# Two-bank PSUM tiles, 64-key post-mix matmuls and new planned durations in a talking-heads attention and MoE kernel

## The chip, the cores and the metric

The kernel runs on one core of a Trainium2 chip. The metric is the device time of one execution in microseconds (us); times before are the median of three runs, beside one profiled execution.

## The reference

All arrays are float32. Attention has batch 4, 12 heads, 448 positions, 64 features a head; the two feed-forward layers see 4 x 448 = 1792 tokens of 768 features, with hidden sizes 2048 and 1024.

```python
scores = scale * q @ k.T                                   # per batch and head
scores = einsum('bhij,hg->bgij', scores, w_pre)            # mixed across the 12 heads
attn = exp(scores - max(scores)); attn /= sum(attn) + 1e-9
attn = einsum('bhij,hg->bgij', attn, w_post)               # mixed across the heads again
x = (attn @ v) as [1792, 768]
h = x @ w_in;  x = elu(h) @ w_out                          # first layer, 768 -> 2048 -> 768
h = x @ w_in2; s = h * softmax(h); s = (s - mean) / sqrt(var + 1e-6) * g_ln
out = s @ w_out2                                           # second layer, 768 -> 1024 -> 768
```

## The kernel before

**Attention.** The 448 query rows of each batch are cut into chunks of 4 to 12 groups of 10 rows, 17 chunks in all (`CH`). For a chunk, a *score pair* (`add_score`, L428 to L461) computes the scores of two heads: four 64 x 64-tiled matmuls (L443) into two PSUM banks, one bank a head. Each bank is copied to SBUF by ScalarE or VectorE (L449, tile `sev`), and DMAs (*moves*, L454) bring the rows of all heads together into tile `sp`, so that the heads lie on partitions. A *unit* is two groups; there are 90. For each unit `pre` (L503 to L508) mixes the heads by matmuls into two banks (`pm`, for r = 0 and 1, five query rows each), `top` takes the maximum of each bank (L513, VectorE), `expo` the exponentials with their sums (L518, ScalarE), `guard`, `inv` and `weigh` (L522 to L531) put 1/sum into the post-mix weights `wr`. `post` (L532 to L542) mixes the heads again and transposes: for each of eight blocks of 56 keys (`JC`; the matmul covers 64, so that neighbours overlap by 8), each r and each of the unit's two groups there is one matmul with 64 keys as stationary columns. Its two output banks `po` hold four column blocks q with two partition halves x (block 2q + x). `take` copies them to `at` (L549). When all units of a chunk are done, `AV` multiplies with V: two halves of six heads (L590), 24 matmuls each, into one bank of the `sc` ring; each half is copied (L597) and stored to DRAM (L602, `xs`).

**PSUM.** The eight banks are three rings: `ps_sc` with three banks (score pairs and AV halves), `ps_po` with two, `ps_pm` with three. In chunks 0 and 1 score pairs also borrow `po` and `pm`.

**Order of work.** Attention's instructions are put in order by a list scheduler when the kernel is built (`schedule`, L296 to L352). Each `op` has a rank (a due time), what it depends on, the ring buffers it takes or uses, and a planned duration per engine that may run it. The scheduler takes the engine that can start earliest and on it the ready op of lowest rank; where two engines may do a copy, the one that would be done first, with `DA` added for VectorE against ScalarE. `tail` is the planned delay until another engine sees a result, `bufs` the size of each ring. Ranks come from a plan made of `PRE`, `POST`, `AV`, `SC` and `HID` (L361 to L393). Each engine and each DMA queue then works through its list in order.

**The first feed-forward layer** runs after it: for each of 8 feature groups `fg` and 4 token blocks `tb`, `hid` (two tiles of 18 matmuls, L256), `elu`, and `outp` of the block before (six tiles of 6 matmuls, L743), whose results VectorE adds up (L759). The two first hidden tiles (fg 0, tb 0) are scheduled by the planner as soon as their inputs are there. Hidden tiles take a bank of `ps_sc`, two of each eight one of `ps_h`. The weights of the second layer are decoded meanwhile (`decode`, L154 to L204: load, clamp L170, words, split, store to DRAM scratch `w2s`). These pieces wait in two lists, `urgent` and `later`; `tick` keeps up to three in progress, takes new ones from `urgent` first, and puts some of their steps between the matmul groups. All weights are decoded by the end of tb 2 of the last feature group (`drain(True)`, L788). **The second layer** loads the decoded weights with `w2_load` (L239 to L243): eleven of the 28 pieces in the last feature group, put on `urgent` at L786 behind tb 0, the others before the layer starts.

Of the kernel before, what the change touches and what calls it, by code (L numbers as in the profile page):

```python
# [26 lines left out]
WMAX = 120  # L27
JC = 56
# [10 lines left out]
XB = 2  # L39
# [13 lines left out]
DA = .4  # L53
T0 = 14
# [4 lines left out]
SB = 8  # L59
# [5 lines left out]
def kernel(ctx: ExitStack, tc: tile.TileContext, qa, kt, vt, wpre, wpost,  # L65
# [217 lines left out]
    tail = {"pe": .2, "act": .15, "dve": .15, "pool": .1, "sp": 2.0, "host": 0.0}  # L283
    bufs = {"sc": 3, "pm": 3, "po": 2, "sev": SB, "e": EB, "wr": WB, "st": 4, "kst": 2, "q": 4,
# [76 lines left out]
    PRE, POST, AV, SC, HID = .78, .96, 2.65, .78, 3.64  # L361
# [35 lines left out]
    k_op, q_op, av_op, sc_ev = {}, {}, {}, {}  # L397
# [30 lines left out]
    def add_score(c, h):  # L428
# [3 lines left out]
        ring = ("sc", "po", "pm")[h // 2 % 3] if c == 0 else ("sc", "po")[h // 2 % 2] if c == 1 else "sc"  # L432
        scb, svb = [Buf(ring) for _ in range(2)], [Buf("sev") for _ in range(2)]
# [3 lines left out]
        def mm(e):  # L437
            T[key] = [pools["ps_" + ring].tile([128, 512], F32, tag=ring, name="sc") for _ in range(2)]
            q, k = q_t[c, h // 6], kt_t[b, h]
            for x in range(2):  # L440
                for i in range(2):
                    sl = slice(64 * i, 64 * i + 64)
                    nc.tensor.matmul(T[key][i][64 * x:64 * x + 64, :S], q[sl, h % 6 // 2, 64 * x:64 * x + 64], k[sl, :],  # L443
                                     start=True, stop=True)

        def evac(e, i):
            t = T["sv", c, h + i] = (k0.tile([128, S], F32, name=f"s0_{h + i}") if c == 0 else
                                     sev_p.tile([128, S], F32, tag="sev", name="sev"))
            copier(e)(t, T[key][i][:, :S])  # L449
# [521 lines left out]
```

## Time and profile before

| what | value |
|---|---|
| median of three runs (lowest, highest) | 1116.82 us (1116.71, 1116.92) |
| the profiled execution, its own time | 1114.65 us |
| its span, first to last instruction | 1112.9 us |
| TensorE busy | 1071.1 us (96%) |
| VectorE, ScalarE, GpSimd busy | 724.0, 502.8, 238.3 us |
| mean granted TensorE clock | 0.986 |

A busy TensorE can still wait inside a group of matmuls, since matmuls overlap and their ends are modelled; so shares of busy time say less than the distance between the starts of groups. PE is TensorE's matmuls, PEld its weight loads, DVE VectorE, ACT ScalarE, POOL GpSimd, SP SyncE (its queue issues most DMAs); L with a number is a line of the kernel.

### The profile page before, as it was taken

The page shows a single profiled execution, that of the slowest core. Times are in us where ns is not written, and L with a number is a line of the kernel's source. Part 1 is how long each engine was busy: PE and PEld are TensorE (multiplying, and loading weights), DVE is VectorE, ACT ScalarE, POOL GpSimd, SP SyncE. Part 2 cuts the span into 40 slices and gives each one's busy share as a digit, 9 for nine tenths or more (in the row PEclk, how much of TensorE's full clock was granted, in tenths as well). Part 3 has the DMA queues.
Part 4 walks back from the last instruction along what each step waited for, and adds up shares of the span by engine and source line. Part 5 has one row for each costly group of instructions (what it writes and reads, how often), then busy time and mean ns, then how long its engine had stood idle before and what let it go on. Part 6 is the DMA issues. An engine that isn't in the chain of part 4 may idle for free.

```text
span 1112.9 us, 29821 instructions
## 1 busy us (share of the span) xinstructions
PE 1071.1 (96%) x12520; PEld 906.6 (81%) x12520; DVE 724.0 (65%) x1394; ACT 502.8 (45%) x1066; POOL 238.3 (21%) x251
## 2 busy tenths in 40 slices
PE   7899999999999899999999999999969999999998
PEld 2576667667776798998989999999969899898988
DVE  5586786677687457688878887878744553443532
ACT  3575677577675365333333434333321343333422
POOL 3210010011012325343344434333412000000000
PEclk8999999999999999999999999999999999999999
DMA  6775775775755432415234242424160600000001
GB/s 198 198 218 174 205 238 170 208 223 167 243 163 163 130 107 94 151 58 170 95 121 140 95 138 76 151 77 151 58 250 16 244 30 15 29 15 29 22 22 43
DMA packets 80232, 141.76 MB, mean 127 GB/s; under 512 B 21019, under 2 KB 59780, under 8 KB 80098
## 3 DMA queue, kind: packets, MB, share of 16 engines
q1 hardware_dynamic: 78275, 136.48, 38.5%
q0 software_dynamic: 896, 1.90, 0.7%
q8 instruction: 98, 1.61, 0.6%
q10 hardware_dynamic: 927, 1.48, 0.4%
q14 instruction: 36, 0.29, 0.1%
HBM read 75.96 MB, written 25.17 MB: 91 GB/s over the span
## 4 chain that ended last, share of the span: by engine, by line
PE 76%; DVE 10%; DMA 7%; issue 3%; ACT 3%; POOL 1%; SPq 0%; DVEq 0%; POOLq 0%; ACTq 0%
PE h L256 14%; PE o L743 14%; PE o L886 11%; PE h L839 11%; PE po L541 7%; PE sc L443 6%; PE pm L508 6%; PE av L590 6%; DMA sp<-sev 3%; DMA ws<-in_wo_dram 2%; DVE x L759 2%; DVE wy L184 1%; DMA ws<-in_wi_dram 1%; DVE wq L180 1%; PE tr L870 1%
## 5 line engine op out<-in xcount | busy, mean ns | idle before, releaser
L513 DVE TENSOR_REDUCE st<-pm 128x1 f32<-128x448 f32 x180 | 107.2, 617 | 72.5 <-PE pm L508 71.1
L743 PE MATMUL o<-gh,woh 128*128 128x448 f32 x384 | 142.2, 370 | 12.1 <-DVE x L759 10.2
L541 PEld LDWEIGHTS po<-wr,e 60*64 60x64 f32 x5760 | 115.2, 136 | 40.6 <-issue 26.6
L518 ACT ACTIVATE e<-pm,st 128x448 f32<-128x448 f32 x180 | 113.5, 634 | 65.2 <-DVE st L513 47.7
L743 PE MATMUL o<-gh,wol 128*128 128x448 f32 x384 | 140.7, 367 | 0.0
L743 PE MATMUL o<-glo,woh 128*128 128x448 f32 x384 | 140.7, 366 | 0.0
L269 POOL TENSOR_TENSOR glo<-g,gh 128x448 fp32r<-128x448 f32 x64 | 83.0, 1297 | 233.8 <-issue 125.1
L443 PE MATMUL sc<-kt,q 64*64 64x448 f32 x816 | 120.6, 564 | 4.6 <-DMA kt<-in_kt_dram 4.3
L541 PE MATMUL po<-wr,e 60*64 60x60 f32 x5760 | 118.9, 221 | 5.8 <-ACT at L549 2.6
L886 PE MATMUL o<-w,lh 128*128 128x384 f32 x448 | 120.3, 340 | 0.0
L508 PE MATMUL pm<-sp,wpre_t 64*64 64x448 f32 x720 | 107.9, 574 | 9.2 <-DMA sp<-sev 5.5
L839 PE MATMUL h<-w,x2h 128*128 128x512 f32 x336 | 107.7, 395 | 0.0
L759 DVE TENSOR_TENSOR x<-x,o 128x448 f32<-128x448 f32 x168 | 101.3, 611 | 8.7 <-PE o L743 8.7
L256 PE MATMUL h<-xh,wih 128*128 128x448 f32 x288 | 106.2, 369 | 0.0
L256 PE MATMUL h<-xl,wih 128*128 128x448 f32 x288 | 105.6, 367 | 0.0
L256 PE MATMUL h<-xh,wil 128*128 128x448 f32 x288 | 105.4, 366 | 0.0
L264 ACT ACTIVATE t<-t 128x448 f32<-128x448 f32 x64 | 37.0, 578 | 134.4 <-DVE t L263 134.4
L529 POOL TENSOR_TENSOR wr<-wpost_t,st 128x120 f32<-128x120 f32 x88 | 35.1, 399 | 288.7 <-DVE st L525 224.8
L590 PEld LDWEIGHTS av<-at,v 128*64 128x64 f32 x1632 | 76.2, 138 | 18.2 <-issue 6.6
L743 PEld LDWEIGHTS o<-gh,woh 128*128 128x128 f32 x384 | 72.6, 189 | 21.4 <-DVE x L759 13.1
L590 PE MATMUL av<-at,v 128*64 128x120 f32 (+5 forms) x1632 | 83.4, 259 | 6.4 <-ACT sev L449 3.3
L549 DVE COPY at<-po 128x480 f32<-128x480 f32 (+1 forms) x119 | 74.6, 649 | 14.9 <-PE po L541 14.1
(98 smaller groups left out, 1949.1 us busy)
## 6 DMA issues: line engine op xcount, KB each, us to landing
sp<-sev SPq DMA_DIRECT2D x94, 210.0 KB
ws<-in_wi_dram SPq DMA_DIRECT2D x33, 512.0 KB
ws<-in_wo_dram SPq DMA_DIRECT2D x21, 512.0 KB
q<-in_qa_dram SPq DMA_DIRECT2D x34, 192.0 KB
v<-in_vt_dram SPq DMA_DIRECT2D x24, 256.0 KB
w2s<-ws SPq DMA_DIRECT2D x12, 512.0 KB
ws<-in_wo_dram SPq DMA_DIRECT2D x16, 384.0 KB
w2s<-ws SPq DMA_DIRECT2D x16, 384.0 KB
```

Source lines behind the costliest of these rows:

```text
L256: nc.tensor.matmul(ps[:, :S], a[:, kc * FG + ft * 128:kc * FG + (ft + 1) * 128], x[:, kc, :], start=kc == 0 and n == 0, stop=kc == ECH - 1 ...
L269: nc.gpsimd.tensor_tensor(glo, g, f(gh), ALU.subtract)
L443: nc.tensor.matmul(T[key][i][64 * x:64 * x + 64, :S], q[sl, h % 6 // 2, 64 * x:64 * x + 64], k[sl, :], start=True, stop=True)
L508: nc.tensor.matmul(ps_t[u][r][64 * s:64 * s + 64, :S], wpre_t[p, :], sp_t[c][p, g, :], start=True, stop=True)
L513: nc.vector.tensor_reduce(out=st_t[u][:P, r:r + 1], in_=ps_t[u][r][:P, :S], op=ALU.max, axis=AX.X, negate=True)
L518: nc.scalar.activation(out=t[:P], in_=ps_t[u][r][:P, :S], func=AF.Exp, bias=st[:P, r:r + 1], scale=1.0, accum_out=st[:P, 2 + r:3 + r])
L541: nc.tensor.matmul(out[:, :, 5 * r:5 * r + 5], e_t[u, r][sl, j:j + 64], wr_t[u][sl, r].rearrange("p (g a) -> p g a", a=5), start=True, sto ...
L590: nc.tensor.matmul(ps[64 * k:64 * k + 64, i, :], v_t[CH[c][0]][:, 6 * n + 2 * i + k, q, :], at_t[c][:, q, 6 * n + 2 * i + k, :w], start=q ...
L743: nc.tensor.matmul(ps[:, :S], a[:, ft * DM + e * 128:ft * DM + (e + 1) * 128], x, start=n == 0, stop=n == 5)
L759: nc.vector.tensor_tensor(x1[tb][:, e, :], x1[tb][:, e, :], ps[:, :S], ALU.add)
L839: nc.tensor.matmul(ps[:, hf * 512:hf * 512 + 512], a[:, k, :], w, start=n == 0, stop=n == 3 * ECH - 1)
L886: nc.tensor.matmul(ps[:, :384], a[:, k, :], w, start=n == 0, stop=n == 3 * FC - 1)
```

## The change

- `post` works on seven blocks of 64 keys in place of eight overlapping ones: blocks 0 to 5 lie in column blocks q = 0 to 2 as before; block 6 is computed for r = 0 in partition half 0 and for r = 1 in half 1 of q = 3. The other places of q = 3 are zero from two memsets at the start, and V's last block holds the same keys in both halves. `po` is two fixed tiles instead of a ring.
- A score pair is one tile of two banks, and the ring `sc` holds one such tile. From chunk 1 on the pair is emptied by one copy into one `sev` tile for two heads (four of these instead of eight of one head). Chunk 0 uses the rings `sc`, `pm`, `pm` and copies head by head; chunk 1 uses `sc` alone.
- `pm` holds two tiles of two banks; one maximum instruction covers both.
- Both AV halves of a chunk go to one `sc` tile, with one copy and one store (`XB` from 2 to 1 buffer of double size).
- The first two hidden tiles take one `pm` tile and wait for the last `pre`; all others use a ring `ps_h` of four banks.
- Planned durations, `tail`, `DA`, the rings' sizes and V's first due times are new. Moves of chunks 0 and 1 may go to SP's or ScalarE's queue, those of chunk 2 to SP's or GpSimd's (before: chunk 0 SP or GpSimd, chunk 1 all three, chunk 2 SP or GpSimd).
- The eleven early `w2_load` go to the end of `later` instead of `urgent`.

```diff
-JC = 56
...
-XB = 2
+XB = 1
...
-DA = .4
+DA = 0
...
-SB = 8
+SB = 4
...
-    ps_sc = pool("ps_sc", 3, space=PSUM)
-    ps_po = pool("ps_po", 2, space=PSUM)
-    ps_pm = pool("ps_pm", 3, space=PSUM)
+    ps_sc = pool("ps_sc", 1, space=PSUM)
+    ps_po = pool("ps_po", 1, space=PSUM)
+    po_p = [ps_po.tile([128, 512], F32, name=f"po{i}") for i in range(2)]
+    ps_pm = pool("ps_pm", 2, space=PSUM)
...
-            ring, p = ("sc", ps_sc) if (tb, ft) not in ((1, 1), (3, 1)) else ("h", ps_h)
-            h_t[fg, tb, ft] = p.tile([128, 512], F32, tag=ring, name="h")
+            if (fg, tb) != (0, 0):
+                h_t[fg, tb, ft] = ps_h.tile([128, 512], F32, tag="h", name="h")
+            elif ft == 0:
+                t = ps_pm.tile([128, 2, 512], F32, tag="pm", name="h")
+                h_t[0, 0, 0], h_t[0, 0, 1] = t[:, 0], t[:, 1]
         ps = h_t[fg, tb, ft]
...
-    tail = {"pe": .2, "act": .15, "dve": .15, "pool": .1, "sp": 2.0, "host": 0.0}
-    bufs = {"sc": 3, "pm": 3, "po": 2, "sev": SB, "e": EB, "wr": WB, "st": 4, "kst": 2, "q": 4,
+    tail = {"pe": .3, "act": .2, "dve": .17, "pool": .1, "sp": 2.0, "host": 0.0}
+    bufs = {"sc": 1, "pm": 2, "po": 2, "sev": SB, "e": EB, "wr": WB, "st": 4, "kst": 2, "q": 4,
...
-    PRE, POST, AV, SC, HID = .78, .96, 2.65, .78, 3.64
+    PRE, POST, AV, SC, HID = .76, .83, 2.6, .76, 3.64
...
-        ring = ("sc", "po", "pm")[h // 2 % 3] if c == 0 else ("sc", "po")[h // 2 % 2] if c == 1 else "sc"
-        scb, svb = [Buf(ring) for _ in range(2)], [Buf("sev") for _ in range(2)]
+        ring = ("sc", "pm", "pm")[h // 2 % 3] if c == 0 else "sc"
+        scb, svb = Buf(ring), Buf("sev")
...
-            T[key] = [pools["ps_" + ring].tile([128, 512], F32, tag=ring, name="sc") for _ in range(2)]
+            T[key] = pools["ps_" + ring].tile([128, 2, 512], F32, tag=ring, name="sc")
...
+            t = T["sv", c, h + i] = k0.tile([128, S], F32, name=f"s0_{h + i}")
+            copier(e)(t, T[key][:, i, :S])
...
+        def evac(e):
+            t = sev_p.tile([128, 2, S], F32, tag="sev", name="sev")
+            T["sv", c, h], T["sv", c, h + 1] = t[:, 0], t[:, 1]
+            copier(e)(t, T[key][:, :, :S])
...
+                o2 = op(r + .9 + .1 * i, lambda e, i=i: evac0(e, i), [o1], [], [scb], act=.43, dve=.54)
...
+                o2 = op(r + .9, evac, [o1], sv, [scb], act=.8, dve=1.0)
...
-                sp_op.setdefault(c, []).append(op(r + 2 + .2 * i + .1 * n, lambda e, i=i, to=to: move(e, i, *to), [o2], [spb_[c]], sv, lag=3.5, sp=.78, **({"act": .78} if c == 1 else {}), **({"pool": 1.0} if c < 3 else {})))
+                sp_op.setdefault(c, []).append(op(r + 2 + .2 * i + .1 * n, lambda e, i=i, to=to: move(e, i, *to), [o2], [spb_[c]], sv if c else [], lag=3.5, sp=.78, **({"act": .78} if c < 2 else {"pool": 1.0} if c == 2 else {})))
...
+    for t in po_p:
+        nc.vector.memset(t, 0.0)
...
-        pmb, pob = [Buf("pm") for _ in range(2)], [Buf("po") for _ in range(2)]
+        pmb, pob = Buf("pm"), [Buf("po") for _ in range(2)]
...
-            ps_t[u] = [ps_pm.tile([128, 512], F32, tag="pm", name="pm") for _ in range(2)]
+            ps_t[u] = ps_pm.tile([128, 2, 512], F32, tag="pm", name="pm")
...
-        def top(e, r, u=u, P=P):
-            if r == 0:
-                st_t[u] = pools["st"].tile([128, 8], F32, tag="st", name="st")
-            nc.vector.tensor_reduce(out=st_t[u][:P, r:r + 1], in_=ps_t[u][r][:P, :S], op=ALU.max, axis=AX.X, negate=True)
+                    nc.tensor.matmul(ps_t[u][64 * s:64 * s + 64, r, :S], wpre_t[p, :], sp_t[c][p, g, :], start=True, stop=True)
+
+        def top(e, u=u, P=P):
+            st_t[u] = pools["st"].tile([128, 8], F32, tag="st", name="st")
+            nc.vector.tensor_reduce(out=st_t[u][:P, 0:2], in_=ps_t[u][:P, :, :S], op=ALU.max, axis=AX.X, negate=True)
...
-            ps = po_t[u] = [ps_po.tile([128, 512], F32, tag="po", name="po") for _ in range(ns)]
-            for q in range(4):
-                for r in range(2):
-                    for x in range(2):
-                        j = min((2 * q + x) * JC, S - 64)
-                        for s in range(ns):
-                            sl = slice(64 * s, 64 * s + 60)
-                            out = ps[s][64 * x:64 * x + 64, q * 120:q * 120 + 120].rearrange("p (g a) -> p g a", a=10)
-                            nc.tensor.matmul(out[:, :, 5 * r:5 * r + 5], e_t[u, r][sl, j:j + 64],
-                                             wr_t[u][sl, r].rearrange("p (g a) -> p g a", a=5), start=True, stop=True)
+
+
+            ps = po_t[u] = po_p
+            for todo in [[(r, 2 * q + x, q, x) for x in range(2)] for r in range(2) for q in range(3)] + [[(0, 6, 3, 0), (1, 6, 3, 1)]]:
+                for r, n, q, x in todo:
+                    for s in range(ns):
+                        sl = slice(64 * s, 64 * s + 60)
+                        out = ps[s][64 * x:64 * x + 64, q * 120:q * 120 + 120].rearrange("p (g a) -> p g a", a=10)
+                        nc.tensor.matmul(out[:, :, 5 * r:5 * r + 5], e_t[u, r][sl, 64 * n:64 * n + 64],
+                                         wr_t[u][sl, r].rearrange("p (g a) -> p g a", a=5), start=True, stop=True)
...
-        for r in range(2):
-            ot = op(r0 + .9 + .1 * r, lambda e, r=r, top=top: top(e, r), [o], [] if r else [sb], [pmb[r]] + ([sb] if r else []), dve=.62)
-            ex.append(op(r0 + 1.6 + .8 * r, lambda e, r=r, expo=expo: expo(e, r), [ot], [eb[r]], [pmb[r], sb], act=.84))
+        ot = op(r0 + .9, top, [o], [sb], [pmb], dve=1.0)
+        ex = [op(r0 + 1.6 + .8 * r, lambda e, r=r, expo=expo: expo(e, r), [ot], [eb[r]], [pmb, sb], act=.63) for r in range(2)]
+        o = op(r0 + 3.2, guard, ex, [], [sb], dve=.07)
+        o = op(r0 + 3.3, inv, [o], [], [sb], dve=.07)
+        ow = op(r0 + 3.4, weigh, [o, o_wpost], [wb], [sb], dve=.3, pool=.38)
...
-                                [pob[s]] + ([at_b[c]] if g else []), act=.58, dve=.64))
+                                [pob[s]] + ([at_b[c]] if g else []), act=.45, dve=.57))
...
-                ov.append(op(t_av[c, 0] - VD + 4 * i if b else T0 + 5 + 2 * i, lambda e, i=i, load=load: load(e, i), [o_begin], [] if i else [vb], [vb] if i else [], sp=.5, lag=4.0))
+                ov.append(op(t_av[c, 0] - VD + 4 * i if b else T0 + 8 + 2.5 * i, lambda e, i=i, load=load: load(e, i), [o_begin], [] if i else [vb], [vb] if i else [], sp=.5, lag=4.0))
+        xb, avb = Buf("x"), Buf("sc")
+
+        def mm(e, n, c=c, w=w):
+            if n == 0:
+                x_t[c] = ps_sc.tile([128, 2, 512], F32, tag="sc", name="av")
...
+        def take(e, c=c, w=w):
+            T["x", c] = pools["xt"].tile([128, 2, 3, WMAX], F32, tag="x", name="x")
+            copier(e)(T["x", c][:, :, :, :w], x_t[c][:, :, :3 * w].rearrange("p n (k w) -> p n k w", k=3))
...
-            o = op(r + AV + .2, take, [o], [xb], [avb], act=.45, dve=.5)
-            T["xs", c, n] = op(r + AV + 1, store, [o], [], [xb], sp=.5, more=.2)
+            o = op(t_av[c, n], lambda e, n=n, mm=mm: mm(e, n), at_ops[c] + ov + [o], [] if n else [avb], [vb, at_b[c]] + ([avb] if n else []), pe=AV * w / 120)
+        o = op(t_av[c, 1] + AV + .2, take, [o], [xb], [avb], act=.68, dve=.78)
+        T["xs", c, 0] = T["xs", c, 1] = op(t_av[c, 1] + AV + 1, store, [o], [], [xb], sp=.5, more=.2)
...
+    hb, o = Buf("pm"), None
     for ft in range(2):
-        o = None
         for p in range(3):
             o = op(t_hid + HD + ft * .01, lambda e, ft=ft, p=p: hid(0, 0, ft, range(2 * p, 2 * p + 2)),
-                   need + [o] + [sc_ev[lc, h] for h in range(NH)], pe=HID / 3)
+                   need + [o, pre_op[NU - 1]], [hb] if (ft, p) == (0, 0) else [], [hb], pe=HID / 3)
...
-    release("ps_pm", "ps_po")
+    release("ps_pm", "ps_po", "ps_sc")
...
-    ps_h = pool("ps_h", 1, space=PSUM)
+    ps_h = pool("ps_h", 4, space=PSUM)
...
-                    urgent.append([(0, lambda i=i: w2_load(i, p), 0)])
+                    later.append([(0, lambda i=i: w2_load(i, p), 0)])
...
-    vb = v.reshape(NB, NH, 4, 2, JC, D)
+    vb = v.reshape(NB, NH, 7, 64, D)
     for n in range(8):
-        o = 8 if n == 7 else 0
-        vt[:, n % 2, o:o + JC, :, n // 2] = vb[:, :, n // 2, n % 2].transpose(0, 2, 1, 3)
+        vt[:, n % 2, :, :, n // 2] = vb[:, :, min(n, 6)].transpose(0, 2, 1, 3)
```

## Rows read from the trace of the kernel before

**Rows 1.** Windows by stage: us, busy us and instructions of each engine, clock, DMA share, GB/s.
```profile
60.00:350.00 290.00, 282.00 (x7527) 205.47 (x7518) 211.93 (x535) 190.94 (x510) 30.92 (x78) 0.99 0.66 199
350.00:395.00 45.00, 39.73 (x683) 34.15 (x683) 25.41 (x42) 20.42 (x44) 15.72 (x12) 0.92 0.42 124
395.00:810.00 415.00, 411.64 (x2025) 378.83 (x2024) 326.24 (x534) 165.09 (x292) 165.09 (x124) 1.00 0.34 113
```

**Rows 2.** Chain that ended last, 232 to 256 us: start, us, what.
```profile
...
237.04 2.61 PE av L590 x48
239.65 0.91 PE pm L508 x8
240.56 0.93 PE po L541 x64
241.49 0.76 PE sc L443 x8
...
253.94 1.03 PE po L541 x63
```

**Rows 3.** Timeline of TensorE, 230 to 256 us; six score pairs, the first to the last.
```profile
241.31 0.94 PE L443 MATMUL sc<-kt,q 64*64 64x448 f32 x8
...
248.63 0.93 PE L443 MATMUL sc<-kt,q 64*64 64x448 f32 x7
...
250.00 1.23 PE L443 MATMUL sc<-kt,q 64*64 64x448 f32 x5
...
252.97 1.06 PE L443 MATMUL sc<-kt,q 64*64 64x448 f32 x8
...
254.90 1.35 PE L590 MATMUL av<-at,v 128*64 128x120 f32 x22
```

**Rows 4.** Groups by shape over the whole span: count, busy us, mean ns, idle before.
```profile
L541 PE MATMUL po<-wr,e 60*64 60x60 f32 x5760 | 118.9, 221 | 5.8 <-ACT at L549 2.6 <-issue 2.1 <-POOL wr L529 0.8
L518 ACT ACTIVATE e<-pm,st 128x448 f32<-128x448 f32 x180 | 113.5, 634 | 65.2 <-DVE st L513 47.7 <-DVE st L525 15.4 <-DVE st L522 1.9
L449 ACT COPY sev<-sc 128x448 f32<-128x448 f32 x129 | 65.3, 536 | 29.6 <-PE sc L443 11.3 <-DMA sp<-sev 8.9 <-DVE sev L449 2.4
L449 DVE COPY sev<-sc 128x448 f32<-128x448 f32 x63 | 38.7, 620 | 7.5 <-PE sc L443 5.2 <-ACT sev L449 1.1 <-ACT e L518 0.4
...
L848 DVE TENSOR_REDUCE s<-h 128x1 f32<-128x1024 f32 x14 | 17.1, 1224 | 77.4 <-PE h L839 77.4
L849 ACT ACTIVATE raw<-h,s 128x1024 f32<-128x1024 f32 x14 | 15.7, 1119 | 21.8 <-DVE s L848 21.6
```

**Rows 5.** Waits of TensorE's weight loads, 60 to 350 us: us, times, longest.
```profile
PEld sc L443 <- ACT sev L449: 6.5, 13, 1.1
```

**Rows 6.** Timeline of TensorE, 819 to 840 us, around its longest stop.
```profile
834.47 0.74 PE L743 MATMUL o<-gh,woh 128*128 128x448 f32 x1 [8.79 <-DVE x L759]
...
839.12 0.57 PE L256 MATMUL h<-xh,wih 128*128 128x448 f32 x1
```

**Rows 7.** Timeline of SP's queue, 780 to 840 us.
```profile
811.62 7.84 SPq L242 DMA_DIRECT2D w<-w2s  x11
820.42 0.33 SPq L161 DMA_DIRECT2D ws<-in_wo_dram  x1
```

**Rows 8.** Timeline of VectorE, 811 to 840 us.
```profile
830.32 0.36 DVE L170 TENSOR_SCALAR ws<-ws 128x384 f32<-128x384 f32 x1 [11.15 <-DMA ws<-in_wo_dram]
```

**Rows 9.** Timeline of all engines, 0 to 32 us.
```profile
1.93 4.54 DVE L470 MEMSET sp<- 128x5376 f32 x1 [1.93 <-issue]
4.27 14.02 PE L443 MATMUL sc<-kt,q 64*64 64x448 f32 x96 [4.27 <-DMA kt<-in_kt_dram]
```

**Rows 10.** Windows of undisturbed scores, and of the stop near 825 us.
```profile
300.00:340.00 40.00, 40.00 (x1134) 29.98 (x1132) 29.81 (x76) 26.99 (x72) 4.64 (x12) 1.00 0.57 174
820.00:830.00 10.00, 5.68 (x29) 4.92 (x27) 0.00 (x0) 0.00 (x0) 1.05 (x1) 0.97 1.01 405
830.00:840.00 10.00, 5.53 (x16) 4.94 (x17) 6.18 (x12) 2.72 (x5) 2.12 (x2) 0.52 0.12 47
```

More of the change, by code (lines that the diff above doesn't have):

```diff
@@ L442, in mm, with evac0 @@
                     sl = slice(64 * i, 64 * i + 64)
-                    nc.tensor.matmul(T[key][i][64 * x:64 * x + 64, :S], q[sl, h % 6 // 2, 64 * x:64 * x + 64], k[sl, :],
+                    nc.tensor.matmul(T[key][64 * x:64 * x + 64, i, :S], q[sl, h % 6 // 2, 64 * x:64 * x + 64], k[sl, :],
                                      start=True, stop=True)
[L446 to L449, printed above, removed]
+        def evac0(e, i):
+            t = T["sv", c, h + i] = k0.tile([128, S], F32, name=f"s0_{h + i}")
[4 more added lines that the diff above has]
+            copier(e)(t, T[key][:, :, :S])
         def move(e, i, p, r0, r1):
@@ L507, in pre @@
                     p = slice(64 * r, 64 * r + 64)
-                    nc.tensor.matmul(ps_t[u][r][64 * s:64 * s + 64, :S], wpre_t[p, :], sp_t[c][p, g, :], start=True, stop=True)
-        def top(e, r, u=u, P=P):
-            if r == 0:
-                st_t[u] = pools["st"].tile([128, 8], F32, tag="st", name="st")
-            nc.vector.tensor_reduce(out=st_t[u][:P, r:r + 1], in_=ps_t[u][r][:P, :S], op=ALU.max, axis=AX.X, negate=True)
+                    nc.tensor.matmul(ps_t[u][64 * s:64 * s + 64, r, :S], wpre_t[p, :], sp_t[c][p, g, :], start=True, stop=True)
+        def top(e, u=u, P=P):
+            st_t[u] = pools["st"].tile([128, 8], F32, tag="st", name="st")
+            nc.vector.tensor_reduce(out=st_t[u][:P, 0:2], in_=ps_t[u][:P, :, :S], op=ALU.max, axis=AX.X, negate=True)
         def expo(e, r, u=u, P=P):
@@ L517, in expo @@
             t = e_t[u, r] = pools["e"].tile([128, S], F32, tag="e", name="e")
-            nc.scalar.activation(out=t[:P], in_=ps_t[u][r][:P, :S], func=AF.Exp, bias=st[:P, r:r + 1], scale=1.0,
+            nc.scalar.activation(out=t[:P], in_=ps_t[u][:P, r, :S], func=AF.Exp, bias=st[:P, r:r + 1], scale=1.0,
                                  accum_out=st[:P, 2 + r:3 + r])
@@ L579 @@
             for i in range(6):
-                ov.append(op(t_av[c, 0] - VD + 4 * i if b else T0 + 5 + 2 * i, lambda e, i=i, load=load: load(e, i), [o_begin], [] if i else [vb], [vb] if i else [], sp=.5, lag=4.0))
-        for n in range(2):
-            r = t_av[c, n]
-            xb, avb = Buf("x"), Buf("sc")
-            def mm(e, c=c, n=n, w=w):
-                ps = x_t[c, n] = ps_sc.tile([128, 512], F32, tag="sc", name="av")[:, :3 * w].rearrange("p (k w) -> p k w", k=3)
-                for i in range(3):
-                    for q in range(4):
-                        for k in range(2):
-                            nc.tensor.matmul(ps[64 * k:64 * k + 64, i, :], v_t[CH[c][0]][:, 6 * n + 2 * i + k, q, :], at_t[c][:, q, 6 * n + 2 * i + k, :w],
-                                             start=q == 0, stop=q == 3)
-            o = op(r, mm, at_ops[c] + ov, [avb], [vb, at_b[c]], pe=AV * w / 120)
-            def take(e, c=c, n=n, w=w):
-                T["x", c, n] = pools["xt"].tile([128, 3, WMAX], F32, tag="x", name="x")
-                copier(e)(T["x", c, n][:, :, :w], x_t[c, n])
-            def store(e, c=c, n=n, w=w):
-                b, r, _ = CH[c]
-                dst = xs[b][n * 384:n * 384 + 384, r:r + w]
-                dma(dst.rearrange("(k p) w -> p k w", k=3), T["x", c, n][:, :, :w])
-            o = op(r + AV + .2, take, [o], [xb], [avb], act=.45, dve=.5)
-            T["xs", c, n] = op(r + AV + 1, store, [o], [], [xb], sp=.5, more=.2)
@@ new lines @@
+                ov.append(op(t_av[c, 0] - VD + 4 * i if b else T0 + 8 + 2.5 * i, lambda e, i=i, load=load: load(e, i), [o_begin], [] if i else [vb], [vb] if i else [], sp=.5, lag=4.0))
[3 more added lines that the diff above has]
+                x_t[c] = ps_sc.tile([128, 2, 512], F32, tag="sc", name="av")
+            for i in range(3):
+                for q in range(4):
+                    for k in range(2):
+                        h = 6 * n + 2 * i + k
+                        nc.tensor.matmul(x_t[c][64 * k:64 * k + 64, n, i * w:i * w + w], v_t[CH[c][0]][:, h, q, :], at_t[c][:, q, h, :w],
+                                         start=q == 0, stop=q == 3)
```

21 lines of the change are left out of this document (11 added, 10 removed).

## The prediction

> **What bounds the kernel now.** I read the table of windows first, since it splits the span by stage. From 60 to 350 us (attention) TensorE is busy 282 of 290 us, and from 395 to 810 us (the first feed-forward layer) 411.6 of 415; for long it stands idle only in 350 to 395 us, 5.3 us [rows 1], and once near 825 us, 8.8 us [rows 6]. In attention DMA has a share of 0.66, VectorE is busy 212 and ScalarE 191 of the 290 us, so none of these is full. A busy TensorE may still be one that is held up inside a group, so I read the chain of waits next: each group of matmuls starts where the one before it ended, av 2.61 us, pm 0.91, po 0.93, sc 0.76 [rows 2]. This stretch is bound by what TensorE has to issue, and a matmul taken away there is time gained, as long as no new wait appears. Third, the timeline of TensorE between two AV blocks shows how close the score pairs follow each other, because the change gives them one buffer in place of three banks. Last, I followed the idle time near 825 us from engine to engine.
>
> **Post-mix, 64 instead of 56 keys for each matmul.** The list of a unit goes from 4 x 2 x 2 x 2 = 32 matmuls to 7 x 2 x 2 = 28. The trace holds two instructions for each (5760 = 90 units x 64 [rows 4]), so 8 of 64 go. The chain takes 0.93 us for 64 [rows 2], 14.5 ns each; 8 x 14.5 ns x 90 units = 10.5 us. Bounds: 0 if the posts wait for weights or for a buffer whatever their number, and 11.8 us at the rate of the slower groups (1.03 us for 63 [rows 2], 16.3 ns x 8 x 90). I take 10.5: 0.93 is what a group takes that waits for nothing. AV still runs over four key blocks of 128 rows: its count does not change.
>
> **The score ring, three banks to one two-bank tile.** Before, a pair's two banks are emptied side by side, 0.536 us on ScalarE and 0.620 on VectorE [rows 4]. Afterwards one instruction empties 2 x 448 columns. The trace has none of this shape; its bounds are one 448-column copy and the 1024-column passes over a two-bank tile, 1.119 us on ScalarE and 1.224 on VectorE [rows 4]. Between these, VectorE needs 0.620 + 448 x (1.224 - 0.620)/576 = 1.09 us; ScalarE, with the slope of its own exps from 0.634 to 1.119, needs 0.536 + 448 x 0.842 ns = 0.91 us. The last matmul of a pair ends 0.94 us after the first one starts [rows 3]; with the copy that is 1.85 to 2.03 us, and with 0.2 us for the two handovers (my estimate, from the 0.15 us by which pm, right after an AV group, is longer in the chain than sc [rows 2]) a pair holds the only tile for 2.05 to 2.25 us. Six pairs start between 241.31 and 252.97 us [rows 3], 2.33 us apart in the mean: on average they fit. But the spacing is uneven: 248.63 and 250.00 are 1.37 apart, and the AV block follows the last pair by 1.93 us. Stretching two such spacings by 0.8 us and the last by 0.3 costs 1.9 us a chunk, 30 us over 16 chunks, if TensorE has nothing else to do in these gaps. The other end is 0: the planner orders by readiness, and each chunk has five or six pre and post groups of 0.8 us to put there. The row nearest to it is what TensorE's weight loads waited for score copies with three banks, 6.5 us in 13 waits [rows 5]. I take as much again, +6.5 us. Queued behind a waiting score matmul are the next pre and post, as TensorE takes its list in order; who waits for these are the VectorE maxima, and through them the copies, so a wait is handed on. For AV, both halves now share the score tile: it is held 5.2 us of matmuls and one copy of 720 columns, between 0.54 and 1.12 us by the same two rows, and the pre and post that follow an AV half (0.91 + 0.93 us) cover the copy. If that cover is gone it costs about 1 us a chunk, within the 30.
>
> A rule of the Trainium skill speaks against this part: "TensorEngine Tiling (Array Packing)", section "PSUM Bottleneck", says that packed matmuls leave the emptying of PSUM as the limit, and asks for both ScalarE and VectorE on it. The rows agree so far as one engine alone takes 0.91 us or more where two in parallel took 0.62. By the rule the sum would lie at the bad end, with 30 us in place of 6.5. [...]
>
> **Maxima, exps and copies.** One maximum over 896 columns (1.09 us by the slope above) replaces two of 448, at most 0.62 each if they cost what the VectorE copy of that shape does [rows 4]: 0.15 us less per unit at most, on an engine that is not full [rows 1]. I cost it at nothing; the first exp of a unit starts some 0.5 us later, and is hidden by the three units that pre runs ahead. The pm ring goes from three banks to two pairs, which removes the wait of a unit's second bank; nothing is counted for it.
>
> **W2 loads from the urgent list to the end of the later one.** Here TensorE stands from 825.7 to 834.47 us, 8.79 us, for an addition on VectorE [rows 6]. VectorE sat 11.15 us before a clamp at 830.32, waiting for a weight load; that load was issued at 820.42 on SP's queue, behind eleven W2 loads that took SP from 811.62 to 819.46 and fill the DMA engines (share 1.01 in 820 to 830 us) [rows 7, 8, 10]. Afterwards the last spill's load goes ahead of these eleven. Then TensorE restarts at the lower clock level: the 12 matmuls from 834.47 to 839.12 take 4.65 us [rows 6] where 12 at 0.203 (411.6 us for 2025 of them [rows 1]) take 2.44. Together 8.8 + 2.2 = 11.0 us. Bounds 0 (another late load takes the wait's place) and 11.0. I take 10. Late next are the W2 loads: eleven of 512 KB are 5.8 MB, 14 us at the 405 GB/s of that window [rows 10]. In the code they are wanted only after hid(7,3) and two more output groups, at the pace of rows 1 some 20 us after the stop's end, so they have cover; past that each costs its own 1.3 us.
>
> **Start and tail.** Two memsets of 128x512 by VectorE's 4.54 us for 128x5376 [rows 9] are 0.4 us each, in front of the first copies: +0.5 (0 to 1). Chunks 0 and 1 score twelve pairs in 14.0 us [rows 9] over all three rings; now chunk 1 has the one tile, 6 x 2.2 = 13.2 us by itself: +2 (0 to 4), since pre waits for the moves' DMA anyway. These 26 moves leave GpSimd's queue for SP and ScalarE, whose copies queue behind an issue (planned at 0.78 us): 0, give or take 3. At the tail the first hidden tiles use the pm ring and need the last pre; that stage's 5.3 us of idle [rows 1] can move by 3 either way. The first layer's four-bank h ring changes a stage where TensorE is 99% busy: 0. New planned durations shift every due time (0.02 + 0.13 us a unit, 0.02 a pair, 0.05 an AV half: about 17 us less in all); loads issue earlier, on an SP queue with room: 0, give or take 4.
>
> **Sum.** -10.5 + 6.5 - 10 + 0.5 + 2 = -11.5 us. The profiled execution took 1114.65 us (span 1112.9 and 1.75 around it), 2.2 below the median of 1116.82; the difference is taken off the median: 1105.
>
> **The rivals.**
> *The ring costs nothing.* The planner fills the gaps, and shorter copies take waits out of the chain. For it: mean spacing 2.33 against 2.25 needed. Both gains in full and start and tail even: 1116.8 - 10.5 - 11 = 1095. Chance 0.22.
> *The ring is the bound.* Place: the score stretch of each chunk; it decides from the point where pair plus copy exceeds the spacing that pre and post leave, about 2.3 us. A copy that queues 0.3 us behind an exp is enough. Full price 30: 1116.8 - 10.5 - 10 + 30 + 2.5 = 1129, the case reaching from 1118 up. Chance 0.15; the 1.37 us spacings speak for it, the mean against it.
> *The gains do not arrive.* Attention is held by the moves into sp instead (DMA share 0.66 [rows 1]), so fewer post matmuls only lengthen waits, or another late load takes the W2 wait's place: with one of the two gains lost and the ring's price, 1115, between 1111 and 1118. Chance 0.15.
> *The clock.* Waits of the ring could bring TensorE to its lower level. From 300 to 340 us, where score waits occur, the granted clock was 1.00; it was 0.52 after the 8.8 us stop [rows 10]. One fall per chunk at the 2.2 us of the W2 stop is 16 x 2.2 = 35 us, from 1105 to 1140. Chance 0.03. The Trainium skill, "TensorE: Matmul & The Clock Gate", section "A second HAM failure mode: psum-queue depth-cycling", says that cycling through PSUM banks can idle TensorE often enough for its clock to swing; this trace shows no such swing with sub-microsecond waits.
>
> **How the numbers follow.** The forecast of 1105 (its own range 1099 to 1111) has 0.45. A change under 0.2% (2.2 us) can't be told from none here. Faster, below 1114.6: 0.45 + 0.22 and about a third of the third rival, 0.72; the same: 0.09, from that rival; slower: the ring, the clock and what is left, 0.19. The range from 1091 to 1121 leaves out the clock, most of the ring's case and the best end of the first rival, near 0.18.
>
> **What would show it.** Right: 5040 post instructions, near 0.82 us a unit in the chain; TensorE's weight loads wait 10 to 15 us for score copies in attention; its stop near 825 us is gone, and W2 is loaded before the second layer starts. Wrong: waits of sc or av for score copies of 20 us or more with TensorE's idle share in attention rising; spacing of score pairs over 2.4 us; a clamp on VectorE that still waits for a weight load; second-layer matmuls waiting for W2; the first post-mix later than before by over 4 us.

## The result, and the profile after

The changed kernel took 1128.87 us (median), against 1116.76 for the kernel before in the same comparison: ratio 1.0112, 95% interval 1.0082 to 1.0142. It is slower by about 12.5 us, where 11.5 us faster was forecast; the range ended at 1121.

The profiled execution spans 1129.0 us, 16.1 more than that of before (1112.9); the medians lie 12 apart. A landmark splits it: the first output matmul (`o`), which opens the stretch of the first feed-forward layer, started at 392.6 us before and starts at 420.3 now. All of the loss lies ahead of it, +27.7 us; from there to the end it is 708.8 us in place of 720.3, so 11.5 are gained. The windows by stage, with one more in which the eleven W2 loads run now (us, busy us and instructions of each engine, clock, DMA share, GB/s):

```profile
0.00:60.00 60.00, 41.05 (x596) 18.02 (x598) 27.37 (x40) 25.42 (x52) 11.23 (x18) 0.83 0.64 185
60.00:350.00 290.00, 257.60 (x6255) 167.49 (x6254) 175.17 (x378) 175.35 (x417) 27.53 (x71) 0.96 0.62 182
...
395.00:810.00 415.00, 411.35 (x2266) 377.18 (x2261) 320.31 (x524) 163.53 (x290) 167.45 (x124) 1.00 0.35 118
...
840.00:860.00 20.00, 20.00 (x100) 18.54 (x99) 10.16 (x19) 5.01 (x10) 4.57 (x4) 1.00 0.95 358
```

In attention TensorE's idle time rose from 8.0 us [rows 1] to 32.4, while every other engine and the DMA share fell: no engine became full. TensorE's granted clock fell too, to 0.96 from 0.99 [rows 1], and in the first 60 us, where before had 0.91, to 0.83. The stop near 825 us is gone [rows 6, 10]: TensorE has no idle time from 810 to 880 us. Groups by shape, 60 to 350 us (count, busy us, mean ns, idle before and what ended it):

```profile
L446 PE MATMUL sc<-kt,q 64*64 64x448 f32 x603 | 83.3, 565 | 9.0 <-ACT sev L456 8.5 <-DVE sev L456 0.4
L520 PE MATMUL pm<-sp,wpre_t 64*64 64x448 f32 x568 | 81.9, 582 | 14.5 <-DMA sp<-sev 5.0 <-ACT e L529 4.4 <-DMA kt<-in_kt_dram 1.7
L552 PE MATMUL po<-wr,e 60*64 60x60 f32 x3920 | 78.1, 220 | 6.3 <-issue 3.1 <-DVE at L560 2.6 <-DVE st L533 0.4
L524 DVE TENSOR_REDUCE st<-pm 128x2 f32<-128x896 f32 x71 | 76.8, 1086 | 52.3 <-PE pm L520 49.6 <-POOL wr L540 2.0
L456 ACT COPY sev<-sc 128x896 f32<-128x896 f32 x50 | 45.8, 915 | 26.2 <-PE sc L446 18.0 <-DMA sp<-sev 6.9 <-ACT e L529 0.7
L456 DVE COPY sev<-sc 128x896 f32<-128x896 f32 x25 | 27.1, 1084 | 0.9 <-PE sc L446 0.3 <-issue 0.2
```

The long copies cost what was worked out (0.91 and 1.09 us). Of the 32.4 us only 9.0 stand in front of score matmuls; 14.5 stand in front of pre-mixes, for score moves, exps and loads. The weight loads' waits for score copies, the number by which the ring was priced [rows 5], are 14.8 us (us, times, longest):

```profile
PEld sc L446 <- ACT sev L456: 12.2, 13, 2.7
...
PEld sc L446 <- DVE sev L456: 2.6, 7, 0.6
```

How one chunk runs now, TensorE from 255 to 285 us; [rows 3] is a chunk of before:

```profile
260.85 5.14 PE L599 MATMUL av<-at,v 128*64 128x120 f32 x96
...
267.69 1.26 PE L520 MATMUL pm<-sp,wpre_t 64*64 64x448 f32 x8 [0.73 <-DMA sp<-sev]
268.46 1.24 PE L446 MATMUL sc<-kt,q 64*64 64x448 f32 x8
...
274.00 0.93 PE L446 MATMUL sc<-kt,q 64*64 64x448 f32 x8
...
276.54 0.98 PE L446 MATMUL sc<-kt,q 64*64 64x448 f32 x8 [0.81 <-ACT sev L456]
...
278.10 0.99 PE L552 MATMUL po<-wr,e 60*64 60x60 f32 x56
278.91 0.94 PE L446 MATMUL sc<-kt,q 64*64 64x448 f32 x8
...
283.69 1.55 PE L599 MATMUL av<-at,v 128*64 128x120 f32 x26
```

Both AV halves run as one block of 5.14 us; the first score pair follows 7.61 us after the block's start, and six pairs, 2.5 us apart in the mean, fill the 15.2 us to the next block. From the first matmul to the end of its copy, AV has the tile for 5.94 us and the pairs have it for 2.07 to 2.65 us each, 13.7 together: 19.7 of the 22.8 us from block to block. The longest free piece, 1.7 us, follows AV's copy; the next pair stands in TensorE's list behind a pre-mix that waits for a move. ScalarE shows AV's copy, and why a pair takes more than matmuls and copy:

```profile
266.03 0.76 ACT L604 COPY x<-av 128x720 f32<-128x720 f32 x1 [2.79 <-PE av L599]
...
274.97 0.63 ACT L529 ACTIVATE e<-pm,st 128x448 f32<-128x448 f32 x1 [0.81 <-DVE st L524]
275.50 0.19 ACT L529 ACTIVATION_READ_ACCUMULATOR e<-pm,st 128x1 f32 x1
275.60 0.90 ACT L456 COPY sev<-sc 128x896 f32<-128x896 f32 x1
```

The pair begun at 274.00 has ended at 274.93; its copy stands behind an exp until 275.60, ends at 276.50, and at 276.54 the next pair starts.

Longer lines for the tile reach the clock. TensorE's timeline, and the windows around it:

```profile
307.49 0.98 PE L446 MATMUL sc<-kt,q 64*64 64x448 f32 x8 [1.07 <-ACT sev L456]
310.40 1.40 PE L446 MATMUL sc<-kt,q 64*64 64x448 f32 x8 [1.93 <-ACT sev L456]
```
```profile
305.00:310.00 5.00, 2.15 (x29) 0.46 (x20) 1.35 (x4) 2.33 (x4) 0.00 (x0) 1.00 0.78 221
310.00:315.00 5.00, 3.17 (x16) 1.00 (x20) 0.36 (x1) 1.53 (x3) 0.00 (x0) 0.58 0.56 182
315.00:320.00 5.00, 4.54 (x28) 1.17 (x21) 3.12 (x4) 2.24 (x7) 0.00 (x0) 0.74 0.62 198
```

TensorE was busy 2.15 of 5 us, held up by score copies, and was then granted 0.58 in the mean of the next 5 us, near the lower of its two levels, 1.2 GHz of 2.4.

### The profile page after: what moved, and what is told of

The parts are those of the page before. It is cut to its first block, busy times and chain, and to the rows that moved or that the text cites. A ratio compares the mean times of both kernels' runs of the same rounds, so it can differ in the third digit from the quotient of the medians.

```text
span 1129.0 us, 28116 instructions
## 1 busy us (share of the span) xinstructions
PE 1065.6 (94%) x11800; PEld 879.2 (78%) x11800; DVE 700.9 (62%) x1255; ACT 502.0 (44%) x1001; POOL 236.2 (21%) x246
## 4 chain that ended last, share of the span: by engine, by line
PE 56%; DVE 11%; DMA 5%; issue 3%; ACT 3%; SPq 1%; POOL 1%; DVEq 0%; POOLq 0%; ACTq 0%
PE h L259 14%; PE o L752 14%; PE o L895 10%; PE h L848 10%; PE av L599 2%; DMA sp<-sev 2%; PE pm L520 2%; DMA ws<-in_wo_dram 2%; DVE x L768 2%; DVE st L524 2%; DVE wy L184 1%; PE sc L446 1%; DVE wq L180 1%; PE po L552 1%; PE tr L879 1%
## 5 line engine op out<-in xcount | busy, mean ns | idle before, releaser
L446 PE MATMUL sc<-kt,q 64*64 64x448 f32 x816 | 113.7, 586 | 27.1 <-ACT sev L456 15.3
L524 DVE TENSOR_REDUCE st<-pm 128x2 f32<-128x896 f32 x90 | 97.2, 1086 | 66.9 <-PE pm L520 64.3
L552 PEld LDWEIGHTS po<-wr,e 60*64 60x64 f32 x5040 | 97.7, 138 | 51.2 <-issue 37.8
L520 PE MATMUL pm<-sp,wpre_t 64*64 64x448 f32 x720 | 102.7, 589 | 16.9 <-DMA sp<-sev 5.8
L552 PE MATMUL po<-wr,e 60*64 60x60 f32 x5040 | 100.5, 222 | 9.3 <-DVE at L560 4.6
L560 DVE COPY at<-po 128x480 f32<-128x480 f32 (+1 forms) x99 | 63.4, 649 | 69.3 <-PE po L552 68.7
L599 PE MATMUL av<-at,v 128*64 128x120 f32 (+5 forms) x1632 | 80.1, 258 | 4.0 <-issue 3.2
L895 PEld LDWEIGHTS o<-w,lh 128*128 128x128 f32 x448 | 81.7, 188 | 0.6
```

The lines of the kernel that those rows point to most:

```text
L446: nc.tensor.matmul(T[key][64 * x:64 * x + 64, i, :S], q[sl, h % 6 // 2, 64 * x:64 * x + 64], k[sl, :], start=True, stop=True)
L520: nc.tensor.matmul(ps_t[u][64 * s:64 * s + 64, r, :S], wpre_t[p, :], sp_t[c][p, g, :], start=True, stop=True)
L524: nc.vector.tensor_reduce(out=st_t[u][:P, 0:2], in_=ps_t[u][:P, :, :S], op=ALU.max, axis=AX.X, negate=True)
L552: nc.tensor.matmul(out[:, :, 5 * r:5 * r + 5], e_t[u, r][sl, 64 * n:64 * n + 64], wr_t[u][sl, r].rearrange("p (g a) -> p g a", a=5), start ...
L599: nc.tensor.matmul(x_t[c][64 * k:64 * k + 64, n, i * w:i * w + w], v_t[CH[c][0]][:, h, q, :], at_t[c][:, q, h, :w], start=q == 0, stop=q == 3)
L895: nc.tensor.matmul(ps[:, :384], a[:, k, :], w, start=n == 0, stop=n == 3 * FC - 1)
```

## The experiments

Ratios are to the kernel before, on the same chip, with 95% intervals; 0.001 is 1.1 us.

**W2 loads alone**, on the kernel before:

```
-                    urgent.append([(0, lambda i=i: w2_load(i, p), 0)])
+                    later.append([(0, lambda i=i: w2_load(i, p), 0)])
```

> The kernel before with one edit: the eleven W2 loads go to the end of the later list. The forecast counted 11.0 us for it (8.8 us of standing, 2.2 us of slow restart), and the trace of the changed kernel has its first layer and second layer together 11.6 us shorter. If the edit gives that by itself: 1105 to 1107 us, and no stop of TensorE near 825 us. If the gain came from the four-bank h ring instead: 1116 to 1117 us with the stop still there.

Measured: 0.9882 (0.9854 to 0.9910), -13 us. TensorE is busy 20.00 of 20 us from 820 to 840.

**64-key post-mix, and the borrowing that comes with its standing tiles.** Three runs on the kernel before: the post-mix with the poorer borrowing, the borrowing alone, and the post-mix with the late W2 loads. Core of the edits:

```
-        ring = ("sc", "po", "pm")[h // 2 % 3] if c == 0 else ("sc", "po")[h // 2 % 2] if c == 1 else "sc"
+        ring = ("sc", "pm")[h // 2 % 2] if c == 0 else "sc"
...
+            ps = po_t[u] = po_p      # and the 28-matmul list of the change
```

> The kernel before with the 64-key post-mix alone (two fixed po tiles with zeros, V laid out for it, POST planned at 0.84 us; score pairs of chunks 0 and 1 borrow pm only, since po is fixed). If attention is bound by what TensorE issues: 10.5 us less, 1106 us, a little more for the lost borrowing. If fewer post matmuls only lengthen waits: 1115 to 1118 us.

> The kernel before, where the score pairs of chunk 0 alternate between the sc and pm rings only and chunk 1 uses sc alone, as in the 64-key run, with the old post-mix. If the post gain of 10.5 us was there and the lost borrowing hid it: 1125 to 1128 us. If borrowing is worth nothing and fewer post matmuls bring nothing: 1115 to 1118 us.

> The 64-key run with the W2 loads last as well. The W2 edit alone gave 13 us and the 64-key post-mix alone nothing; if they add up: 1102 to 1105 us. If the stop of the W2 loads had hidden the post gain: 1093 to 1097 us.

Measured: 1.0024 (0.9994 to 1.0055), 1.0105 (1.0065 to 1.0145) and 0.9888 (0.9852 to 0.9924). So the post-mix gains about 9 us, and the lost borrowing seemed to cost 12. But the trace of the borrowing alone shows another loss: TensorE's waits from 60 to 300 us name loads of q, of which before has none there:

```profile
PE sc L443 <- DMA q<-in_qa_dram: 7.4, 3, 3.6
PE pm L508 <- DMA q<-in_qa_dram: 6.1, 2, 3.8
```

The planner orders all instructions by simulating the buffers, so any edit of a ring gives a new order of the whole attention, SP's queue included. Two runs take this apart: the banks changed in an order held as before (planned with the old rings), and the new order with q due earlier:

```
+        real = ("sc", "pm")[h // 2 % 2] if c == 0 else "sc"     # tiles from real, plan with ring
```
```
-op(r - 9 if c > 1 else ...
+op(r - 15 if c > 1 else ...
```

> The kernel before with the order of its instructions as it was, planned with the old borrowing; only the banks change: chunks 0 and 1 score into the score ring and, for chunk 0, the maxima's ring, and no longer borrow the post-mix banks. Theory R (the lost banks cost by themselves): about 12 us slower than before, as in the run where the plan was made anew, 1.010. Theory O (the 12 us are of the order that the planner made anew from the changed buffers, and the banks cost next to nothing): within 2 us of before, 0.998 to 1.003.

> The kernel with only the poorer borrowing, planned anew (1.0105), with the loads of q due 6 us earlier from chunk 2 on. In its trace TensorE waited 13.5 us between 60 and 300 us for loads of q that stood late in the SP queue, and before's trace has no such wait. If these waits are the loss: about 11 us back, 0.999 to 1.003. If they only show a loss that is elsewhere (a wait that takes its place): 1.008 or more.

Measured: 1.0011 (0.9992 to 1.0030) and 1.0003 (0.9978 to 1.0028); the waits for q are gone from the second trace. The lost banks cost about 1 us, within the noise; most of the other 11 came of a new order that asked for q too late. A placebo shows how far an order alone carries:

```
-    PRE, POST, AV, SC, HID = .78, .96, 2.65, .78, 3.64
+    PRE, POST, AV, SC, HID = .77, .96, 2.65, .77, 3.64
```

> The kernel before with a pre-mix and a score pair planned at 0.77 us instead of 0.78, and nothing else: a placebo that only shifts due times and so the order of the instructions. If the order matters little: within 3 us of before, 0.997 to 1.003. If the order by itself is worth as much as the effects that are being told apart: off by 5 us or more, either way.

Measured: 0.9964 (0.9938 to 0.9990), 4 us faster for nothing. Differences of 4 us between single orders are therefore not read as effects below.

**Two score banks in place of three**, planned anew and in the order held for three (the third bank serves two hidden tiles of the feed-forward layer alone):

```
-    ps_sc = pool("ps_sc", 3, space=PSUM)
+    ps_sc = pool("ps_sc", 2, space=PSUM)
-    bufs = {"sc": 3, ...
+    bufs = {"sc": 2, ...     # this line only where planned anew
```

> The kernel before, with two banks in the score ring instead of three; the third bank serves hidden tiles alone. Pairs are still emptied by two copies side by side and each AV half still has its own bank. Theory R (what attention lost is that no score pair can be computed while the one before is emptied): much of the loss shows here too, 10 us or more over 1116.5, so 1127 to 1145 us. If the third bank is not what counts: 1114 to 1120 us.

> The kernel before with two score banks in place of three, but in the order planned for three; the third bank serves two hidden tiles after the attention alone. Theory R (a third bank is worth its time by itself): 1.012, as where the order was planned anew for two. Theory O (the order is what costs): within 5 us of before, 1.000 to 1.005. In an order made for three banks each shortage stands on TensorE in line, so a value above 1.012 is possible too and would say that the new plan had saved some of it.

Measured: 1.0124 (1.0088 to 1.0161) and 1.0068 (1.0046 to 1.0089). The bank costs 7.6 us where nothing else moves, and here some 6 more by the new order.

**The changed kernel with one part undone**: two copies of 448 columns for one of 896; the old planned durations; three single banks and two maxima for the pairs of pm; chunk 1 borrowing the pm pairs:

```
-            copier(e)(t, T[key][:, :, :S])
+            copier(e)(T["sv", c, h + i], T[key][:, i, :S])
```
```
-    PRE, POST, AV, SC, HID = .76, .83, 2.6, .76, 3.64     # and DA, tail, the ops' durations
+    PRE, POST, AV, SC, HID = .78, .84, 2.65, .78, 3.64
```
```
-            ps_t[u] = ps_pm.tile([128, 2, 512], F32, tag="pm", name="pm")
+            ps_t[u] = [ps_pm.tile([128, 512], F32, tag="pm", name="pm") for _ in range(2)]
```
```
-        ring = ("sc", "pm", "pm")[h // 2 % 3] if c == 0 else "sc"
+        ring = ("sc", "pm", "pm")[h // 2 % 3] if c < 2 else "sc"
```

> The changed kernel, but from chunk 1 on each score pair is emptied by two copies, one bank each, which may run on ScalarE and VectorE side by side (planned 0.43 and 0.54 us); the ring still holds one tile. Theory R (one score tile, held through one long copy, sets the pace): the tile is held 0.4 us less for each of 96 pairs, so up to 38 us of hold; 10 to 25 us less than 1129, that is 1104 to 1119 us. Theory P (the new planned durations order the work badly): within 4 us of 1129.

> The changed kernel with the plan of before: DA 0.4, the old tails, PRE, AV and SC, durations as one instruction lasts in the trace (exp 0.84, guard and inv 0.16, take 0.58 and 0.64, the pair's copy 0.91 and 1.09, the maximum 1.09, the AV copy 0.76 and 0.91 us), POST 0.84, V's old due times. Theory P: most of the 38 us that attention lost beyond the post gain comes back, 1100 to 1115 us. Theory R: within 5 us of 1129, either way.

> The changed kernel, with pm as three single banks, a maximum and an exp for each (as before); the score tile, the AV tile, the 64-key post-mix, the plan and the W2 order as changed; chunk 0's pairs alternate between sc and pm. Theory Q (TensorE's pre waits for exps, since both pm banks come free together and late): 10 us or more come back, below 1119 us. Theory R (the score tile): within 5 us of 1129.

> The changed kernel with chunk 1's score pairs borrowing the maxima's pairs as chunk 0's do. Theory S (the start costs: six pairs of chunk 1 wait 1.0 to 1.4 us each for the one tile, the first AV ran 14 us later than before): about 8 us faster than the changed kernel, 1121, 1.003. Theory T (the loss is in the steady attention, and a start that is late is caught up, as in the run with the poorer borrowing in a held order): within 3 us of the changed kernel, 1.009 to 1.013.

Measured: 1.0083 (1.0057 to 1.0110), 1.0093 (1.0060 to 1.0127), 1.0110 (1.0075 to 1.0145), 1.0097 (1.0071 to 1.0122). Plan, pm pairs and start are at most 2 us each, within what an order moves; the long copy may be 3, where 10 to 25 were expected if its hold set the pace.

**The change without its pairs**: the kernel before with two score banks, the standing 64-key post tiles, the poorer borrowing and the late W2 loads, AV halves and scores in single banks.

> The changed kernel's counts of banks without its pairs: the kernel before with two score banks, fixed post-mix tiles of 64 keys, the poorer borrowing and the late W2 loads; the AV halves and the scores keep single-bank tiles with a copy each, and the order is planned anew. Measured one at a time these sum to +14 (two banks, planned anew) +2.5 (64-key post-mix with the poorer borrowing) -13 (W2) = +3, 1120, 1.003. Theory U (pairs cost: one long copy, one move later, both AV halves holding both score banks): between 1.000 and 1.005, so 7 to 12 us of the changed kernel's loss are the pairs'. Theory V (the small number of banks costs, whatever the shape of the tiles): 1.009 or more, as the changed kernel.

Measured: 1.0015 (0.9992 to 1.0039). The pairs cost some 11 us, beyond what the placebo moved. In this run the AV halves stand apart, mostly 4 to 6 us from start to start, with other work between:

```profile
260.35 2.68 PE L591 MATMUL av<-at,v 128*64 128x120 f32 x48
266.60 2.68 PE L591 MATMUL av<-at,v 128*64 128x120 f32 x48
```

**AV halves together, and apart.** The first adds the sharing to the run above (both banks taken at the first half, copied out after the second); the other takes it out of the changed kernel (a standing score tile, a bank, copy and store for each half):

```
+            avb = [Buf("sc"), Buf("sc")] if n == 0 else avb
```
```
+                ps = x_t[c, n] = sc_p[:, n, :3 * w].rearrange("p (k w) -> p k w", k=3)
```

> e14 (single-bank tiles, two score banks, 1.0015) with the two AV halves of a chunk taking both score banks at the first half and copied out only after the second, in two copies. Theory W (the shared AV tile is most of what the pairs cost): 6 to 9 us above e14, 1.007 to 1.010. Theory X (what costs is the score pair, its one copy and the moves that wait for it): within 3 us of e14, 0.999 to 1.004.

> The changed kernel with its pair of score banks as one standing tile that a score pair fills and one long copy empties as before, but with each AV half in one bank, with its own copy, its own output tile and its own store. Theory W: 6 to 9 us faster than the changed kernel, 1.003 to 1.006. Theory X: within 3 us of it, 1.008 to 1.013.

Measured: 1.0131 (1.0106 to 1.0156), 13 us above the run without pairs, more than theory W asked; and 1.0103 (1.0058 to 1.0147), nothing gained. The second hardly tested its point: its halves were free to part, but most still stand in one block, probably since a score pair needs both banks:

```profile
260.20 5.14 PE L600 MATMUL scp<-at,v 128*64 128x120 f32 x96
```

In the first the loss shows again on pre-mixes, TensorE's waits from 60 to 350 us beginning with

```profile
PE pm L511 <- DMA sp<-sev: 12.3, 4, 6.3
PE pm L511 <- DMA q<-in_qa_dram: 3.3, 1, 3.3
```

**Asking earlier**, on the changed kernel: q as above, and `SCM = 15` for 12.

> The changed kernel with two due times moved and nothing else: the loads of q 6 us earlier from chunk 2 on, and a chunk's scores due to end 15 us ahead of its first pre-mix instead of 12. Theory L (score moves and loads that come late are most of the loss, as with the poorer borrowing): 6 us or more faster than the changed kernel, 1.006 or less. Theory N (the held tile is the bound, and asking earlier only lengthens the line in front of it): 1.008 or more.

Measured: 1.0167 (1.0126 to 1.0208), worse. The waits for moves grew from 5.0 us to

```profile
PE pm L520 <- DMA sp<-sev: 11.0, 5, 4.9
```

Theory L falls for this kernel. The likely reason, which no run shows by itself: a move waits for its pair's copy, the copy for the pair, the pair for the tile, and an earlier due time only puts other work behind that line.

**A version that beats both**: the kernel before, its order and rings kept, with the late W2 loads and the 64-key post-mix in two `po` tiles taken and zeroed once, after chunk 1's scores gave the banks back:

```
+            if (u, r) == (0, 1):
+                T["po"] = [ps_po.tile([128, 512], F32, tag="po", name="po") for _ in range(2)]
+                for t in T["po"]:
+                    nc.vector.memset(t, 0.0)
```

> The kernel before, in its own planned order with its own rings and borrowing, with two parts of the change: the post-mix of 64 keys in two tiles that are taken and zeroed once, after the first chunks gave the banks back, and the W2 loads at the end of the later list. If both gains add (W2 -13 us, measured alone; post-mix -9 us, by the two runs with the poorer borrowing): about 1095 us, 0.980. If the post-mix gains only where it makes up for the poorer borrowing: that of the W2 loads alone, about 1103 us, 0.988.

Measured: 1092.69 us, 0.9805 (0.9771 to 0.9838): both gains add. TensorE in attention, whose 6 idle us are fewer than before's:

```profile
60.00:350.00 290.00, 284.04 (x7095) 200.81 (x7087) 218.78 (x551) 197.87 (x527) 34.27 (x81) 1.00 0.68 206
```

**The way from there to the change**, by ratio and by the start of the first output matmul in each profile:

| kernel | ratio | first `o`, us | clock shortfall, us |
|---|---|---|---|
| best: W2, post-mix, old rings | 0.9805 | 379.6 | 6.8 |
| poorer borrowing, planned anew | 0.9888 | 391.7 | 6.8 |
| and two score banks | 1.0015 | 403.0 | 3.4 |
| and pairs, two copies (and the change's plan and moves) | 1.0083 | 411.7 | 10.2 |
| the change: one long copy | 1.0112 | 420.3 | 20.5 |

The last column adds (1 - granted clock) x 10 us over the 10-us windows from 0 to 420 us; before has 10.2. It is what the lower level took at most, since work that waits for something else loses nothing by it. The two slowest runs, AV together and asking earlier, have 15.3 and 27.3. These are single executions. Span times (1 - mean granted clock), averaged over all runs of a kernel, gives for the whole execution 6.2, 7.2, 5.2, 15.1 and 16.0 us down the table, and 15.6 for AV together.

## Why the prediction was wrong

**W2 loads** (-10, bounds 0 and 11.0): right in kind; -13 alone (-10 to -16 by the interval), 11.5 us in the changed kernel after the landmark. The load in front of which VectorE stood does come ahead of the eleven.

**Post-mix** (-10.5, 0 to -11.8): right. Groups of 56 follow each other in 0.81 us (278.10 to 278.91) against 0.93 for 64; the whole gives 0.9805/0.9882, -8.7 us.

**The score ring** (+6.5, 0 to +30): the step that failed. From three banks to one pair the table has (0.9888 to 1.0112) +25 us: 14 for the third bank, 11 for the pairs. The copies came out as worked out, 0.91 and 1.09 us, and so did the waits for score copies (14.8 us, forecast 10 to 15) and the hold where a copy found its engine free, 2.19 us from pair to pair at the start:

```profile
12.41 0.98 PE L446 MATMUL sc<-kt,q 64*64 64x448 f32 x8 [1.41 <-ACT s L451]
14.60 1.77 PE L446 MATMUL sc<-kt,q 64*64 64x448 f32 x8 [1.21 <-DVE sev L456]
```

Two things were wrong with the step. It set the hold against the spacing of the six pairs, 2.33 us, as if the tile were free around them; but AV keeps the same tile. Added up over a chunk, the step's own figures (six pairs of 2.05 to 2.25 us, AV's 5.2, its copy of 0.54 to 1.12) are 18.0 to 19.8 us, and in the kernel before two such chunks begin their AV 21.3 us apart, at 254.90 [rows 3] and at

```profile
276.21 2.68 PE L590 MATMUL av<-at,v 128*64 128x120 f32 x48
```

That leaves 1.5 to 3.3 us in a chunk for every copy that stands behind something else, 0.67 us behind an exp in the one above. The sentence that AV's share is covered by the pre and post after it missed this. And the step counted waits of scores alone: a late pair makes late moves, and 14.5 us of the idle time stand before pre-mixes. The step said that a wait is handed on, and gave that no price. Of the signs that the forecast named for being wrong, the wider spacing came (2.5 us against 2.4), the 20 us of score waits did not. That the ring costs 25 us is measured; that it does so along this path is read from one trace. The 14 us of the third bank (7.6 in a held order) come before AV and scores share a pair, and their path was not traced.

**The ring is the bound** was thus the rival that came nearest, down to the copy behind an exp, at 1129; it had 0.15. That its number was met is in part luck: the ring took 25 us and not 30, the start with its new order (below) 9 and not 2.5. *The clock* (0.03) was counted as a case of its own and came as a part of this one: in the profiles the shortfall is 20.5 us against 10.2 before, so up to 10 us, where one fall for each chunk was priced at 35. By the averages over all runs it sets in with pairs (5.2, then 15.1 and 16.0), so the clock can be most of what the pairs cost; without pairs, two banks have no more of it than three (5.2 against 7.2), so it is not what the third bank costs. No run here holds it fixed. The forecast gave it little because 300 to 340 us of before showed no fall; here waits of 1.07 and 1.93 us stand right ahead of one. The section on psum-queue depth-cycling in the page "TensorE: Matmul & The Clock Gate" of the Trainium skill, which the forecast set aside, agrees with these rows so far as idle time between groups of matmuls goes with a clock that swings. The other two rivals fell: the ring costs, and both gains arrived.

**Start and tail** (+2 for the one tile, others near 0): the second term that was too small. The parts that were priced hold: the lost banks cost 1 us in a held order, and lending to chunk 1 gives 1.7 back, both within the noise. What the part left out is that new rings make a new order: 9 us in the table (0.9805 to 0.9888), 11 us in the run with the borrowing alone, most of it late q loads, and 4 us the other way in the placebo. "0, give or take 4" was said of new durations and not of new rings. The forecast is 24 us short: 18.5 by the ring, 7 by this, less 1.3 by which the two gains came out larger (21.8 for 20.5).

**Maxima, exps and copies** (0): pm pairs for single banks, no difference (1.0110 against 1.0112).

Open: how the 11 us of the pairs divide, between lines in front of the tile and the clock that they bring down; TensorE's idle time from 60 to 350 us rises with them too, from 21.1 us without pairs to 32.4 in the change. Adding the shared AV tile to single banks cost 13, taking it out of the changed kernel nothing, as its halves stayed together; two copies gave back 3, within what an order moves. Whether an order could be found that parts AV and scores in one pair was not tried.

## What to carry to other kernels

A buffer that loses its spare is priced by its occupancy over a whole period, every user counted, against the length of that period: near full, queueing delays are paid, they show on other instructions than the ones that wait for the buffer, and the gaps can go with a lower clock. Where a planner orders the instructions, an edit of a resource should be run twice, in the old order and in a new one, beside a placebo, before a difference is put down to the resource. A bundle is worth taking apart: two of its parts alone beat it by 34 us (0.9805 against 1.0112).
